# Routing the first batch in two groups of two head pairs, loading the next batch's q and k on the Pool queue, and eight buffers for the split of q and k, in a fused attention and feed-forward kernel

## The chip, the cores and the metric

The kernel runs on one core of one Trainium2 chip. The metric is the device time of one execution in microseconds (us). The kernel before took 321.93 us here (median of 4 executions, 321.57 to 322.32); in the rounds of the experiments its executions lay between 319.6 and 324.6. An execution counts as slow when it lies more than 1.5% above the fastest of its kernel, and as fast otherwise. Most are fast; the slow ones are up to five of the 20 or so of a run (e9, e13, e14, e15, e18), and the profiles of e9, e15 and e18 fell on one, which is said where it matters. The span of a profile is about 1.8 us shorter than the time of the same execution, and the profiled execution of the kernel before was one of its slower ones (323.8 us, span 322.0).

## The reference, cut to what matters

q, k and v are 4 x 8 x 768 x 64 (batches, heads, rows, columns). Each row of q and of k goes to the nearest of 16 centroids of its head; a query sees only keys of its own cluster. The result passes through a feed-forward layer of width 2048. Some lines are drawn together here.

```python
q_assign = np.argmax(np.einsum('bhsd,hcd->bhsc', q_n, c_n), axis=-1)
k_assign = np.argmax(np.einsum('bhsd,hcd->bhsc', k_n, c_n), axis=-1)
mask = q_assign[:, :, :, None] == k_assign[:, :, None, :]
scores = np.where(mask, scale * np.matmul(q, k.transpose(0, 1, 3, 2)), -1000000000.0)
...                                    # softmax
attn_out = np.matmul(attn, v)
h = x @ w_in                           # x: attn_out as 3072 x 512
out = (h * (1.0 / (1.0 + np.exp(-h)))) @ w_out
```

## The kernel before

The work is cut into pieces: 16 pairs of heads (four per batch), three thirds of the queries each. For every pair q and k are loaded (`nat`), split into a high and a low half of 16 bits (`hl`), and turned (`abt`): the first batch on TensorE, the later ones by a DMA transpose on the SP queue. TensorE computes the centroid logits (`psL`), VectorE turns them, takes the maximum and writes one-hots (`lt`, `mx`, `oht`, `ohu`), and these go as extra rows under q and k, so that one product gives the score and the mask at once (`st`). ScalarE takes the exponential (`P`), TensorE multiplies by v (`pv`), VectorE normalises (`xh`), and the feed-forward layer follows (`ph`, `tn`, `gt`, `po`). Four head pairs of one third make a chunk (12 in all).

The order of instructions on every engine isn't written out. The kernel holds a list scheduler that runs when it is built: each piece has a planned duration, a rank, buffers that it takes and gives, and for a DMA a planned landing. Whatever is ready first in this plan is emitted first, and the chip then runs each engine strictly in that order.

```python
    def split_hi(p, t, eng):
        hl = hls[p, t] = mp.tile([128, 2 * NJ, 2, D], f16, name="hl", bufs=5)
    ...
    def route_put(p, h, t, eng):               # one-hots under q or k, 16 rows a head
        g = 64 * h + 32 * t
        dst, src = heads(p, t)[D : D + HC, h], ohs[p][g : g + HC, :]
    ...
    def qk(n, s, p, u):
        K = D + HC                             # 64 + 16 rows
        st = sts[n, s] = ps.tile([128, 2, 2, UQ], f32, name="st", tag="st", bufs=2)
    ...                                        # in the scheduler
                x = min(can, key=lambda x: x.rank if e == "PE" else x.rank + x.t)
                x.fn(ENG[e])                   # emit it
    ...
    for pl in [[p] for p in range(HB)] + [[p, p + 1] for p in range(HB, NP, 2)]:
        groups[pl[-1]] = pl                    # first batch: four groups of one pair
    ...
            x = Piece({"SP": 0.5}, lambda e, p=p, t=t: load(p, t), ...)
    ...
                turned[p].append(Piece(
                    {"SP": 1.45}, lambda e, p=p, t=t: turn_dma(p, t), [los[t]], ..., dma=(1.9 * RATE, 2.0),
                ))
```

The logits of a group take one of the two score buffers (tag `st`), the same two through which every product of scores passes.

The softmax here doesn't subtract the row's maximum and nothing guards it: scores larger than these inputs give would overflow.

Of the kernel before, what the change touches and what calls it, by code (L numbers as in the profile page):

```python
# [19 lines left out]
def kernel(  # L20
# [43 lines left out]
    wlx = const.tile([128, HB * 64 + 32], f16, name="wl")  # L64
    wh, wl = (w[:, 0 : HB * 64].rearrange("p (r h c) -> p r h c", h=2, c=32) for w in (whx, wlx))

    NV = 6
# [12 lines left out]
    def load(p, t):  # L80
        b, r = divmod(p, HB)
        nat = mp.tile([128, 2, NJ * D], f32, name=f"nat{t}", bufs=3)
        nc.sync.dma_start(nat, (q, k)[t][b, 2 * r : 2 * r + 2].rearrange("h (p j) d -> p h (j d)", j=NJ))
        nats[p, t] = nat
# [6 lines left out]
    def split_hi(p, t, eng):  # L91
        hl = hls[p, t] = mp.tile([128, 2 * NJ, 2, D], f16, name="hl", bufs=5)
# [37 lines left out]
    def logits(pl):  # L130
        tl = []
        for lo, hi in ((0, 512), (512, 768)):
# [6 lines left out]
            if pl[0] >= HB:  # L139
# [59 lines left out]
    def route_put(p, h, t, eng):  # L199
        g = 64 * h + 32 * t  # L200
        dst, src = heads(p, t)[D : D + HC, h], ohs[p][g : g + HC, :]
        if eng is nc.scalar:
            eng.mul(dst, src, OHV)  # L203
        else:
            eng.tensor_scalar(out=dst, in0=src, scalar1=OHV, scalar2=None, op0=ALU.mult)  # L205

    def qk(n, s, p, u):
        K = D + HC
# [129 lines left out]
    def centroid_norm():  # L338
        newton()
        newton()  # L340
        nc.vector.tensor_scalar(out=cy, in0=cy, scalar1=1e-6, scalar2=None, op0=ALU.add)
        nc.vector.reciprocal(cw, cy)

    def centroid_split():
        cn = mp.tile([128, D], f32, name="cn")
        nc.gpsimd.tensor_scalar(out=cn, in0=craw, scalar1=cw, scalar2=OHV, op0=ALU.mult, op1=ALU.mult)

        for n in range(2):
            nc.gpsimd.tensor_copy(ch2[:, n, :], cn)
        for n in range(2):  # L350
            nc.gpsimd.tensor_tensor(out=cl2[:, n, :], in0=cn, in1=ch2[:, n, :], op=ALU.subtract)
# [13 lines left out]
    BUFS = {"nat0": 3, "nat1": 3, "hl": 5, "abt": 7, "moe": 3, "po": 1, "lt": 1, "mx": 1, "oht": 1, "ohu": 1, "oh": 2,  # L365
# [3 lines left out]
    RATE = 0.375  # L369
# [17 lines left out]
    def run(free):  # L387
# [3 lines left out]
        jobs, flowed, turn = {"SP": [], "POOL": []}, 0.0, 0  # L391
# [5 lines left out]
        for at in sorted(set(free.values())):  # L397
            post(at)

# [11 lines left out]
        def flow(new=None):  # L411
            nonlocal flowed, turn
            busy = [q for q in jobs.values() if q]
            for q in busy:
                q[0][0] -= (t - flowed) * RATE / len(busy)
# [7 lines left out]
            if busy:  # L423
                turn += 1
                post(t + max(min(q[0][0] for q in busy), 0.0) * len(busy) / RATE, "flow", turn)
# [51 lines left out]
    GAP = 1.7  # L477
    BACK = 6
    SEQ0 = [(0, 0), (0, 1), (1, 0), (2, 0), (3, 0), (1, 1), (2, 1), (3, 1), (0, 2), (1, 2), (2, 2), (3, 2)]
    LEAD, LEAD_V, LEAD_IN = 28, 16, 36  # L480
    FR0 = (-400, -285, -290, -280)
    REX = -300
    LATE = 10
    PSL = 16
    XPE = (0, 11)
    TURNED = (0, 1, 2, 3)


# [11 lines left out]

    def from_slot(x):
# [3 lines left out]
    free = {"PE": 1.0, "ACT": 2.0, "DVE": 1.7, "POOL": 1.3, "SP": 1.2}  # L505
    nc.sync.dma_start(craw, centroids.rearrange("h c d -> (h c) d"))
    nc.vector.memset(zbias, 0.0)
    nc.vector.memset(bias32, -32.0)
    for vt in vts:
        nc.gpsimd.memset(vt[:, :, :, D : D + 1], 1.0)  # L510
    nc.vector.memset(idle, 0.0)
    make_identity(nc, ident)
# [4 lines left out]
    x = Piece({"SP": 0.01}, lambda e: None, rank=-99, dma=(0.0, 1.2))  # L517
    x = Piece({"DVE": 0.45}, lambda e: centroid_square(), [x], rank=-9)
    x = Piece({"ACT": 0.3}, lambda e: centroid_root(), [x], rank=-900)
    Piece({"ACT": 1.28}, lambda e: e.preload_act_table(AF.Exp), [x], rank=-900)  # L520
    x = Piece({"DVE": 1.35}, lambda e: centroid_norm(), [x], rank=-900)
    x = Piece({"POOL": 1.8}, lambda e: centroid_split(), [x], rank=-99)
    cc = [("moe", "c0")]
    x = Piece({"PE": 0.6}, lambda e: centroid_turn(), [x], cc, rank=-99)
# [181 lines left out]
```

## Time and profile before

| | before |
|---|---|
| span of the profile | 322.0 us |
| TensorE (PE) / ScalarE (ACT) / VectorE (DVE) busy | 94% / 74% / 59% |
| needed matmul work, by the prediction's working | 282 us |
| first exponential; first product of the feed-forward layer (ph) | 19.64; 47.68 us |
| first logits of the second batch (psL of pairs 4 and 5) | 66.22 us |

The page cuts the span into 40 slices of 8.05 us. A digit is the busy share of the slice in tenths; PEclk is the granted TensorE clock, DMA the mean busy share of the 16 DMA engines. From the page of the kernel before:

```profile
PE   6688795999999999999989999999999999999994
...
PEclk9799998999999999999999999999999999999999
DMA  7999999999926990394996970293310200200001
```

TensorE is short of work only in the first seven slices, and the DMA engines are at 9 tenths in slices 2 to 11: the place where the change acts is also where DMA is full.

### The profile page before, as it was taken

The page shows a single profiled execution, that of the slowest core. Times are in us where ns is not written, and L with a number is a line of the kernel's source. Part 1 is how long each engine was busy: PE and PEld are TensorE (multiplying, and loading weights), DVE is VectorE, ACT ScalarE, POOL GpSimd, SP SyncE. Part 2 cuts the span into 40 slices and gives each one's busy share as a digit, 9 for nine tenths or more (in the row PEclk, how much of TensorE's full clock was granted, in tenths as well). Part 3 has the DMA queues.
Part 4 walks back from the last instruction along what each step waited for, and adds up shares of the span by engine and source line. Part 5 has one row for each costly group of instructions (what it writes and reads, how often), then busy time and mean ns, then how long its engine had stood idle before and what let it go on. Part 6 is the DMA issues. An engine that isn't in the chain of part 4 may idle for free.

```text
span 322.0 us, 7812 instructions
## 1 busy us (share of the span) xinstructions
PE 302.5 (94%) x3316; PEld 225.5 (70%) x3316; DVE 190.2 (59%) x356; ACT 239.3 (74%) x279; POOL 35.3 (11%) x57
## 2 busy tenths in 40 slices
PE   6688795999999999999989999999999999999994
PEld 4565574876877768777677777777777787786651
DVE  5798983675856878438328877338444344254431
ACT  5896994985678979886878787886787787786420
POOL 4952100024000000023200000040000000000000
PEclk9799998999999999999999999999999999999999
DMA  7999999999926990394996970293310200200001
GB/s 213 289 240 239 235 186 149 214 149 132 223 67 183 210 231 9 77 129 61 191 243 155 223 147 11 75 166 25 69 41 17 66 35 28 74 0 35 33 35 65
DMA packets 89843, 40.00 MB, mean 124 GB/s; under 512 B 75216, under 2 KB 86224, under 8 KB 89808
## 3 DMA queue, kind: packets, MB, share of 16 engines
q1 hardware_dynamic: 62032, 32.16, 44.1%
q0 software_dynamic: 27776, 7.34, 22.8%
q8 instruction: 26, 0.43, 0.6%
q14 instruction: 9, 0.07, 0.1%
HBM read 27.30 MB, written 6.29 MB: 104 GB/s over the span
## 4 chain that ended last, share of the span: by engine, by line
PE 78%; DMA 9%; DVE 9%; ACT 1%; issue 1%; SPq 1%; DVEq 0%
PE ph L276 25%; PE po L298 24%; PE st L213 16%; PE pv L229 9%; DMA abt<-hl 6%; PE psL L155 3%; DMA nat<-in_q_dram 2%; DMA xt<-xh 2%; DVE hl L102 1%; DVE abt L205 1%; DVE ohu L187 1%; DVE lt L162 1%; DVE hl L97 1%; DVE mx L173 1%; DVE oht L180 1%
## 5 line engine op out<-in xcount | busy, mean ns | idle before, releaser
L219 ACT ACTIVATE P<-st,bias 128x1024 f16<-128x1024 f32 x144 | 156.7, 1114 | 36.6 <-PE st L213 36.1
L285 DVE SCALAR_TENSOR_TENSOR gt<-tn,ph 128x512 f16<-128x512 f32 x96 | 65.1, 683 | 61.1 <-ACT tn L282 60.4
L276 PE MATMUL ph<-xt,win_s 128*128 128x256 f16 x768 | 97.1, 274 | 4.1 <-DVE xh L243 3.3
L298 PE MATMUL po<-wout_s,gt 128*128 128x512 f16 x384 | 96.5, 379 | 1.1 <-DVE ot L307 1.1
L213 PE MATMUL st<-abt 80*128 80x256 f16 x576 | 85.5, 274 | 4.0 <-ACT abt L203 1.6
L276 PEld LDWEIGHTS <-win_s 128*128 128x128 f16 x768 | 74.1, 98 | 18.1 <-DVE xh L243 3.6
L282 ACT ACTIVATE tn<-ph,zbias 128x512 f32<-128x512 f32 x96 | 65.3, 686 | 25.3 <-PE ph L276 24.7
L213 PEld LDWEIGHTS <-abt 80*128 80x128 f16 x576 | 55.1, 98 | 26.5 <-issue 3.7
L298 PEld LDWEIGHTS <-gt 128*128 128x128 f16 x384 | 35.9, 97 | 29.1 <-issue 1.6
L89 POOL DMA_DIRECT2D vt<-in_v_dram x32 | 26.5, 833 | 174.0 <-PE pv L229 165.2
L229 PE MATMUL pv<-vt,P 128*128 128x65 f16 x1152 | 43.3, 193 | 0.2 <-ACT P L219 0.2
L229 PEld LDWEIGHTS <-P 128*128 128x128 f16 x1152 | 41.8, 98 | 2.1 <-ACT P L219 0.3
L102 DVE SCALAR_TENSOR_TENSOR hl<-nat,hl 128x768 f16<-128x768 f32 x32 | 29.8, 956 | 2.8 <-ACT hl L95 2.5
L307 DVE TENSOR_SCALAR ot<-po 128x512 f32<-128x512 f32 x24 | 16.5, 686 | 24.2 <-PE po L298 24.1
L242 DVE RECIPROCAL rz<-pv 128x4 f32<-128x4 f32 x48 | 8.6, 178 | 28.0 <-PE pv L229 27.6
L243 DVE TENSOR_TENSOR xh<-pv,rz 128x256 f16<-128x256 f32 x48 | 20.4, 424 | 1.7
L97 DVE TENSOR_SCALAR hl<-nat 128x768 f16<-128x768 f32 x19 | 10.4, 556 | 5.3 <-DMA abt<-hl 5.2
L268 PE MATMUL warm<-idle,ident 128*128 128x256 f16 x66 | 11.7, 316 | 1.7 <-POOL ident masks.py:199 1.7
L95 ACT ACTIVATE hl<-nat 128x768 f16<-128x768 f32 x13 | 11.0, 843 | 2.6 <-DMA nat<-in_q_dram 2.2
L155 PE MATMUL psL<-abt,wh 128*32 128x512 f16 (+1 forms) x128 | 10.5, 340 | 0.7 <-DVE abt L122 0.4
L187 DVE STREAM_TRANSPOSE ohu<-oht 128x768 f16<-128x768 f16 x10 | 9.8, 977 | 0.9 <-DVE oht L180 0.5
L117 PE MATMUL ptt<-ident,hl 128*128 128x128 f16 x96 | 7.7, 235 | 2.7 <-ACT abt L122 1.9
(52 smaller groups left out, 100.4 us busy)
## 6 DMA issues: line engine op xcount, KB each, us to landing
nat<-in_q_dram SPq DMA_DIRECT2D x16, 384.0 KB, 5.2
nat<-in_k_dram SPq DMA_DIRECT2D x16, 384.0 KB, 5.6
out_dram<-ot SPq DMA_DIRECT2D x24, 256.0 KB, 2.1
vt<-in_v_dram POOLq DMA_DIRECT2D x32, 96.0 KB, 5.1
win_s<-in_moe_w_in_dram POOLq DMA_DIRECT2D x4, 512.0 KB, 13.2
wout_s<-in_moe_w_out_dram POOLq DMA_DIRECT2D x4, 512.0 KB, 22.9
abt<-oh SPq DMA_DIRECT2D x48, 24.0 KB, 2.0
abt<-hl SPq DMA_TRANSPOSE x24, 4.5
```

Of the source, the lines that this page charges most:

```text
L89: nc.gpsimd.dma_start(vts[p % NV][:, h, :, 0:D], v[b, 2 * r + h].rearrange("(p j) d -> p j d", j=NJ))
L102: nc.vector.scalar_tensor_tensor(out=hl[:, :, 1, :], in0=nat, scalar=128.0, in1=hl[:, :, 0, :], op0=ALU.mult, op1=ALU.subtract)
L155: nc.tensor.matmul(psL[g : g + 32, 0 : hi - lo], w, x[:, lo:hi], start=first, stop=last)
L213: nc.tensor.matmul(st[:, a, h, :], ab[0:K, 1, h, ts(2 * s + a, 128)], ab[0:K, 0, h, ts(u, UQ)], start=True, stop=True)
L219: nc.scalar.activation(out=P, in_=sts.pop((n, s)), func=AF.Exp, bias=bias32, scale=ESC)
L229: nc.tensor.matmul(out[:, e, h, :], P[:, a, h, ts(e, 128)], vts[p % NV][:, h, 2 * s + a, 0 : D + 1], start=(s + a + h + e == 0), stop=(s = ...
L243: nc.vector.tensor_tensor(out=xhs[c][:, :, r], in0=out[:, :, :, 0:D], in1=rz.unsqueeze(3).to_broadcast([128, 2, 2, D]), op=ALU.mult)
L276: nc.tensor.matmul(ph[:, e].rearrange("p (g x) -> p g x", g=2), win_s[:, r, ts(2 * f + e, 128)], xts[c][:, :, r, :], start=(r == 0), stop= ...
L282: nc.scalar.activation(out=tn, in_=phs[c, f], func=AF.Tanh, bias=zbias, scale=0.5)
L285: nc.vector.scalar_tensor_tensor(out=gts[c][:, 2 * f : 2 * f + 2, :], in0=tns.pop((c, f)), scalar=1.0, in1=phs.pop((c, f)), op0=ALU.add, o ...
L298: nc.tensor.matmul(pos[c, s], gts[c][:, fc, ts(s, 128)], wout_s[:, fc, :], start=(fc == 0), stop=(fc == NFB - 1))
L307: eng.tensor_scalar(out=ot, in0=pos.pop((c, s)), scalar1=0.5, scalar2=None, op0=ALU.mult)
```

## The change

The intent is to take VectorE's routing of the first batch, the wait for a split buffer, and the late start of the next batch's loads out of the first 66 us.

```diff
-    def load(p, t):
+    def load(p, t, eng):
...
-        hl = hls[p, t] = mp.tile([128, 2 * NJ, 2, D], f16, name="hl", bufs=5)
+        hl = hls[p, t] = mp.tile([128, 2 * NJ, 2, D], f16, name="hl", bufs=8)
...
-            if pl[0] >= HB:
+            if len(pl) == 2:
...
-        K = D + HC
+        K = D + (32 if p < HB and len(groups_of[p]) == 2 else HC)
...
-    FR0 = (-400, -285, -290, -280)
+    FR0 = (-295, -295, -285, -280)
-    LEAD, LEAD_V, LEAD_IN = 28, 16, 36
+    LEAD, LEAD_V, LEAD_IN = 18, 22, 23
-    XPE = (0, 11)
+    XPE = (0,)
+    GR0 = [[0, 1], [2, 3]]
...
-                {"SP": 0.5}, lambda e, p=p, t=t: load(p, t), turned[HB - 1] if b == 1 else (), ...
+                {"POOL": 0.75} if b == 1 else {"ACT": 0.45} if p == 0 and t == 1 else {"SP": 0.5}, ...
...
-                    rank=-9 if b == 0 else -2, dma=(1.9 * RATE, 2.0),
+                    rank=-9 if b == 0 else -2, dma=(1.45, 2.0, 0.25),
```

Cut from it: the one-hot writes by 32 rows with a mask (`pick`) that clears the other head's 16 rows of k; the centroids split on ACT and DVE instead of Pool; the value and weight loads moved ahead of the second batch's q and k, with a planned start of 7.8 us (`HOLD`); the order of the first batch's score products (`SEQ0`) and a few smaller ranks and gaps; new figures for the plan's DMA model; and a table of 12 hand-set shifts of rank. `LEAD`, `LEAD_V` and `LEAD_IN` say how many score slots (products of scores, four matmuls each) ahead of its use the splits, values and loads of a later batch may start.

## The prediction

> **What bounds the kernel now.** I read the busy shares first: TensorE (PE) 94%, ScalarE (ACT) 74%, VectorE (DVE) 59% of 322.0 us. So PE is the bound on average, but the 40 slices show its first seven at 6 to 9 tenths. The question is therefore how much of the span is not needed matmul work, and where it lies. The chain of waits gives the warm duration of each group of matmuls:
>
> ```profile
> 60.22 0.88 PE ph L276 x8
> 61.10 0.98 PE st L213 x8
> 64.26 0.86 PE po L298 x4
> 66.29 1.42 PE psL L155 x32
> ...
> 159.14 5.07 DMA xt<-xh
> ...
> 309.29 0.87 PE ph L276 x8
> ```
>
> Columns are start, duration, what. In unbroken stretches eight ph matmuls take 0.873 us, four po 0.866, four st (scores) 0.437, 24 pv 0.735, a routing group psL of 32 takes 1.41. Times the counts: 96 x 0.873 + 96 x 0.866 + 144 x 0.437 + 48 x 0.735 = 265.1 us; routing logits 10.2, PE transposes 6.7. Sum 282 us. So 40 us of the span are not needed work. The timeline of PE says where:
>
> ```profile
> 46.95 0.89 PE L229 MATMUL pv<-vt,P 128*128 128x65 f16 x24
> 47.68 1.04 PE L276 MATMUL ph<-xt,win_s 128*128 128x256 f16 x8
> ...
> 53.31 1.64 PE L276 MATMUL ph<-xt,win_s 128*128 128x256 f16 x8 [3.28 <-DVE xh L243]
> 54.74 1.91 PE L213 MATMUL st<-abt 80*128 80x256 f16 x8
> ```
>
> Up to the first ph at 47.68 the counts in the program order (20 score slots, 6 pv, all of the first batch's transposes and logits) make 22.0 us of work: 25.7 us lost. From there to the next batch's first psL at 66.22, 13.1 us of work take 18.5: 5.4 lost, of which 3.28 is one wait and the rest mostly a cold clock (eight ph in 1.64 us instead of 0.87). From 66.22 to the last po at 318.0, 247.1 us of work take 251.8: 4.7 lost. The last eviction and store take 4.0. Sum 39.8. Hence nearly all that can be won lies before 66 us.
>
> What sets the first ph? The timelines of ACT and DVE:
>
> ```profile
> 19.64 2.12 ACT L219 ACTIVATE P<-st,bias 128x1024 f16<-128x1024 f32 x2
> ...
> 32.00 1.70 ACT L203 ACTIVATE abt<-ohu 16x768 f16<-16x768 f16 x2 [2.43 <-DVE ohu L187]
> 34.29 12.18 ACT L219 ACTIVATE P<-st,bias 128x1024 f16<-128x1024 f32 x12 [0.59 <-PE st L213]
> ```
> ```profile
> 52.14 0.56 DVE L97 TENSOR_SCALAR hl<-nat 128x768 f16<-128x768 f32 x1 [5.25 <-DMA abt<-hl]
> 52.62 0.17 DVE L242 RECIPROCAL rz<-pv 128x4 f32<-128x4 f32 x1
> ```
>
> The first ph comes right after the sixth pv, which needs 18 exponentials. Only 6 are done by 28.87, with ACT copies and routing between them; then ACT waits for DVE's routing of the later pairs, and 12 run without a gap at 1.015 us from 34.29 to 46.47. The first ph follows 1.2 us later. So the first-batch routing on DVE sets when ACT can run, and ACT's exponentials set when the MoE starts. The second fence is the later stall: DVE, in order, holds a split of the next batch for a free buffer (five of them, freed by a DMA transpose issued at 41.03 that lands 11.1 us later), and behind it stand the normalisation and the gates that PE needs.
>
> **What the skill says.** "TensorE: Matmul & The Clock Gate", Part 2, LDWEIGHTS: the time depends on columns, not on contraction rows. The trace agrees: st with 80 rows and ph with 128 both take 274 ns a matmul and 98 ns a load, so 96-row scores cost PE nothing. The same page, Part 1: an idle PE falls to half clock; the cold ph after the 3.28 us wait agrees. "DMA: Bandwidth & Descriptors", Issuing engines are not separate DMA queues: Pool's loads share the same 16 DMA engines, so moving loads brings no bandwidth, only another order. The trace agrees: the engines are at 9 tenths in nearly all of the first 80 us whichever queue moves. "GPSIMD Engine Reference", 2.1: the first call of a freshly loaded Pool kernel costs about 6 us. No run here shows it; it matters below.
>
> **The change part by part.**
>
> Routing in two groups. DVE now does per group lt 1.12 + mx 0.95 + oht 0.95 + ohu 0.98 = 4.0 (the two-pair durations of the second batch), twice, against 1.12 + 0.55 + 0.56 + 0.98 = 3.2 four times: 8.0 for 12.8, so 4.8 us less. The 16 writes of one-hots stay at 0.36 on DVE or 0.84 on ACT, with 32 partitions in place of 16. The price: the first exponential must wait for four tiles, not two. In the new instruction order every first-batch PE transpose copy but the DVE ones is placed on ACT before its first exponential, and after it 20 exponentials stand in one row.
>
> When does that row start? Loads: the third and fourth landed at 8.86 and 9.88, the fifth at 11.0. The new order issues q0 first and k0 beside it on ACT, so I take about 0.4 earlier. ACT splits q2 at 10.6 to 11.5, then four copies at 0.75 to 14.5, another to 15.3, the split of k3 to 16.1, two copies to 17.6; these finish pairs 0 and 1, and psL runs to 19.1. DVE has meanwhile three low splits from 11.5 to 14.4 (0.95 each), two copies, and the high and low splits of k2, k3, q3, to 19.5. Then 4.0 for the routing and the writes of pair 0, 23.5 to 24.7; scores; first exponential about 25.3. That is 5.7 later than now (19.64), but the 18th ends at 25.3 + 18 x 1.015 = 43.6 instead of 46.47. The second group is routed on DVE by 29.7 and its pairs written by 31 and 33.3, before ACT has used up the nine slots of pairs 0 and 1 (34.4): no gap. First ph: 43.6 + 1.2 = 44.8, a gain of 2.9 us.
>
> Eight split buffers. The DVE wait of 5.25 goes, and with it the 3.28 us wait and the cold stretch. From first ph to psL the new order has 12.5 us of work (27 score slots, 7 pv, 8 ph, 2 po) where the old one had 13.1. Walking ACT's 20 exponentials, the tanhs after them (0.69) and the gates (0.68) leaves PE about even: psL near 57.4. But psL also needs four DMA transposes. The low splits end about 43, 46, 48 and 52; a transpose took 4.2 us free and 8.4 to 12.2 among loads, so the fourth lands between 56 and 60. I put 1 us of stall there: 58.4.
>
> Next batch's q and k on Pool. They now queue behind the weights. Weights move at about 0.4 MB/us when alone; 8.4 MB after the values (19 us) end near 40, not 48.6, and q4 lands about 41.5. DVE reaches its split at 39 and has the next normalisation due at 42: just in time. Behind this, the SP queue is free for the transposes. No further gain counted.
>
> Centroid work moved from Pool to ACT and DVE: about 0.4 us and 0.4 us, plus 0.9 us of masks on DVE before the centroids arrive; all in time that DVE and ACT spend waiting for loads. Value loads could start before 7.88. Last chunk turned by DMA: 28 po (6.1 us) stand between its last pv and its first ph, over 0.8 + 3.3 to 5.1 us of normalisation and transpose: hidden.
>
> Sum: psL at 58.4 instead of 66.2, work behind it 247.1 in both, so 7.8 us; 322.2 - 7.8 = 314.4. I say 314.5.
>
> **The rivals.**
> (1) The data hold it up. If Pool starts its value loads at 2 us instead of 7.9, their small packets compete with q and k: between 12 and 18 us the SP queue fell from 0.3 to 0.1 MB/us beside them. The first exponential would slip to 28 or later and the gain at the first ph would be gone: about 317.5. The 6 us of the skill speaks against it, the absence of any wait in the instruction order for it.
> (2) The transposes take the place of the wait. DMA is saturated to about 70 us in the old trace, the bytes stay, and the four transposes landed by 61.1 there. If they do no better now, psL waits to 61 and the time is 317.
> (3) ACT becomes the bound in the first 60 us and all else is hidden well: no stall at psL, weights early, steady part slightly better (no 0.9 us wait for xt as at 164): 312.
>
> **Range and chances.** The first two cost 2.5 to 3 us each and can add up, the third gives 2.5; the later schedule was also reshuffled, worth 1.5 either way. 310.5 to 319 should hold it 8 times in 10. Two per cent is 315.8, only 1.3 above my value: faster 0.62, same 0.36, slower 0.02.
>
> **What would show it.** Right: 20 exponentials in one row on ACT from about 25, first ph near 45, no DVE wait for a DMA transpose, psL of the second batch by 59, and the stretch after that about as long as before. Wrong: value loads landing before 12 us and q1, k1 after 11; a DVE wait for q4 longer than 2 us; a PE wait for abt<-hl before psL; more than 6 us lost after 60 us.

## The result, and the profile after

The changed kernel took 325.15 us (median of 4, 324.81 to 327.0) against 321.93 us in the same rounds. The ratio of the fast runs is 1.0112, with a 95% interval of 1.0070 to 1.0153. A ratio here is the mean time of one kernel's fast runs over that of the other's in the same rounds, so it isn't quite the ratio of the medians. The kernel is 1% slower, inside the 2% band, and 10.6 us above the predicted 314.5; the range of 310.5 to 319.0 doesn't hold it.

The profiled execution was the slowest of the four (327.0 us, span 325.2). A repeat in another call (324.82 us, span 323.0) is used beside it, below as "the repeat". From the page of the changed kernel, the same rows:

```profile
PE   7487999789999999998999999999999999999994
...
PEclk9978799979999999999999999999999999999999
DMA  8999999995092199997473399995120200300301
```

The 5 of slice 7, which was the wait for a split buffer, has become a 9. But slices 2 and 4 are lower than before (4 and 7 for 6 and 8), slices 8 and 9 have 7 and 8 where both had 9, and the clock is low in slices 3 to 5 and 9. DMA is full to slice 9.

The timeline of TensorE. The columns are the start, the duration, the engine, the line, the operation, output and inputs, and in brackets the idle time before it and what ended it:

```profile
27.96 1.05 PE L217 MATMUL st<-abt 96*128 96x256 f16 x8 [1.37 <-DVE lt L164]
...
49.43 1.04 PE L280 MATMUL ph<-xt,win_s 128*128 128x256 f16 x8
...
63.77 0.38 PE L156 MATMUL psL<-abt,wh 128*32 128x512 f16 x1 [1.28 <-DMA abt<-hl]
...
66.51 0.61 PE L156 MATMUL psL<-abt,wh 128*32 128x512 f16 x6 [2.36 <-DMA abt<-hl]
```

The first ph comes at 49.43, not at the predicted 44.8. The logits of pairs 4 and 5 are reached at 62.10, but their group stands on the DMA transposes until 66.51. The timeline of ScalarE, for the row of exponentials:

```profile
26.34 1.11 ACT L223 ACTIVATE P<-st,bias 128x1024 f16<-128x1024 f32 x1
28.61 4.33 ACT L223 ACTIVATE P<-st,bias 128x1024 f16<-128x1024 f32 x4 [1.16 <-PE st L217]
34.00 2.18 ACT L223 ACTIVATE P<-st,bias 128x1024 f16<-128x1024 f32 x2 [1.06 <-PE st L217]
36.56 1.11 ACT L223 ACTIVATE P<-st,bias 128x1024 f16<-128x1024 f32 x1 [0.38 <-PE st L217]
38.03 12.20 ACT L223 ACTIVATE P<-st,bias 128x1024 f16<-128x1024 f32 x12 [0.35 <-PE st L217]
```

The predicted "20 exponentials in one row" are broken four times by 2.95 us in all. The 18th ends at 48.21 (counted from the records; 45.88 in the repeat, 43.6 predicted). The timelines of SP and Pool of the changed kernel, for the transposes and for the first loads:

```profile
48.14 22.55 SPq L113 DMA_TRANSPOSE abt<-hl  x7
```
```profile
1.59 6.76 POOL L90 DMA_DIRECT2D vt<-in_v_dram  x8
```

and SP of the kernel before:

```profile
41.03 1.38 SPq L112 DMA_TRANSPOSE abt<-hl  x1
```

The value loads begin at 1.59 us, where the plan meant 7.8; and the first transpose of the second batch is issued 7 us later than before, though its data (q4) landed at 39.0 us. VectorE's timeline shows both ends of that:

```profile
43.57 0.18 DVE L246 RECIPROCAL rz<-pv 128x4 f32<-128x4 f32 x1 [2.37 <-PE pv L233]
...
44.13 0.55 DVE L98 TENSOR_SCALAR hl<-nat 128x768 f16<-128x768 f32 x1
...
47.16 0.95 DVE L103 SCALAR_TENSOR_TENSOR hl<-nat,hl 128x768 f16<-128x768 f32 x1
...
63.98 0.56 DVE L98 TENSOR_SCALAR hl<-nat 128x768 f16<-128x768 f32 x1 [3.99 <-DMA nat<-in_k_dram]
```

The split of q4 stands behind a normalisation that waits 2.37 us for TensorE, and later a split waits 3.99 us for k7, with gates of the feed-forward layer behind it.

**Where the time went.** All matmul records are in the traces, so a ledger can be made: at a given matmul, the time minus the needed work of all matmuls before it (the prediction's durations times the counts) is the time lost up to there. In us:

| lost up to | before | changed | repeat |
|---|---|---|---|
| first ph | 25.7 | 27.5 | 25.1 |
| 60 us | 30.7 | 27.4 | 26.1 |
| 80 us | 31.2 | 33.8 | 30.6 |
| 160 us | 31.9 | 36.0 | 33.0 |
| last po | 35.9 | 39.6 | 37.4 |

The needed work is 282.2 us before and 281.6 after (one chunk fewer is turned on TensorE). So the changed kernel is 3.3 us ahead at 60 us, and then loses 6.4 us in 20 us where the kernel before loses 0.5, and 5.8 us from 80 us on against 4.7.

### The profile page after: what moved, and what is told of

Same layout as the page of the kernel before. It is cut to its first block, busy times and chain, and to the rows that moved or that the text cites. A ratio compares the mean times of both kernels' runs of the same rounds, so it can differ in the third digit from the quotient of the medians.

```text
span 325.2 us, 7775 instructions
## 1 busy us (share of the span) xinstructions
PE 304.6 (94%) x3309; PEld 227.1 (70%) x3309; DVE 189.3 (58%) x360; ACT 235.9 (73%) x272; POOL 38.3 (12%) x60
## 4 chain that ended last, share of the span: by engine, by line
PE 78%; DMA 9%; DVE 8%; ACT 3%; issue 1%; SPq 0%
PE po L302 24%; PE ph L280 22%; PE st L217 17%; PE pv L233 10%; DMA abt<-hl 6%; PE psL L156 3%; ACT P L223 3%; DMA nat<-in_k_dram 2%; DVE hl L103 2%; DVE gt L289 1%; DVE hl L98 1%; DMA craw<-in_centroids_dram 1%; DVE abt L209 1%; DVE ot L311 1%; DVE lt L163 0%
## 5 line engine op out<-in xcount | busy, mean ns | idle before, releaser
L217 PE MATMUL st<-abt 80*128 80x256 f16 (+1 forms) x576 | 86.4, 277 | 2.6 <-DVE lt L164 1.4
L217 PEld LDWEIGHTS <-abt 80*128 80x128 f16 (+1 forms) x576 | 55.2, 99 | 23.8 <-issue 4.2
L302 PEld LDWEIGHTS <-gt 128*128 128x128 f16 x384 | 36.2, 98 | 31.3 <-issue 2.9
L233 PEld LDWEIGHTS <-P 128*128 128x128 f16 x1152 | 43.2, 99 | 2.3
L233 PE MATMUL pv<-vt,P 128*128 128x65 f16 x1152 | 44.5, 196 | 0.0
L311 DVE TENSOR_SCALAR ot<-po 128x512 f32<-128x512 f32 x24 | 16.6, 690 | 25.7 <-PE po L302 23.2
L156 PE MATMUL psL<-abt,wh 128*32 128x256 f16 (+1 forms) x128 | 11.5, 352 | 5.5 <-DMA abt<-hl 5.3
L272 PE MATMUL warm<-idle,ident 128*128 128x256 f16 x67 | 12.9, 333 | 1.4 <-POOL ident masks.py:199 1.4
L98 DVE TENSOR_SCALAR hl<-nat 128x768 f16<-128x768 f32 x21 | 11.8, 572 | 4.0 <-DMA nat<-in_k_dram 4.0
L123 ACT COPY abt<-ptt 128x768 f16<-128x768 f16 x14 | 10.1, 812 | 2.1 <-PE ptt L118 2.1
L118 PEld LDWEIGHTS <-hl 128*128 128x128 f16 x96 | 6.0, 100 | 7.3 <-DVE hl L103 3.6
```

What stands on the lines that cost most here:

```text
L156: nc.tensor.matmul(psL[g : g + 32, 0 : hi - lo], w, x[:, lo:hi], start=first, stop=last)
L217: nc.tensor.matmul(st[:, a, h, :], ab[0:K, 1, h, ts(2 * s + a, 128)], ab[0:K, 0, h, ts(u, UQ)], start=True, stop=True)
L233: nc.tensor.matmul(out[:, e, h, :], P[:, a, h, ts(e, 128)], vts[p % NV][:, h, 2 * s + a, 0 : D + 1], start=(s + a + h + e == 0), stop=(s = ...
L302: nc.tensor.matmul(pos[c, s], gts[c][:, fc, ts(s, 128)], wout_s[:, fc, :], start=(fc == 0), stop=(fc == NFB - 1))
L311: eng.tensor_scalar(out=ot, in0=pos.pop((c, s)), scalar1=0.5, scalar2=None, op0=ALU.mult)
```

## The experiments

Eighteen kernels ran. All are of three rounds, except the last two of five. "Ratio" is against the kernel before of the same call.

| run | what it is | median us (executions) | ratio, 95% interval |
|---|---|---|---|
| e1_same | changed kernel again | 324.82 (7) | 1.0104, 1.0068 to 1.0140 |
| e2_buf8 | before + eight split buffers | 323.09 (13) | 1.0053, 1.0024 to 1.0081 |
| e3_pool | before + loads on Pool | 328.06 (4) | 1.0217, 1.0172 to 1.0262 |
| e4_groups | before + two groups | 327.55 (4) | 1.0181, 1.0139 to 1.0224 |
| e5_order | changed, splits earlier | 326.36 (4) | 1.0123, 1.0072 to 1.0175 |
| e6_held | changed, values really held | 325.31 (16) | 1.0094, 1.0066 to 1.0121 |
| e7_ring | changed, logits in the other ring | 322.54 (12) | 1.0031, 1.0007 to 1.0055 |
| e8_clear | changed, no loads beside transposes (wrong result) | 327.82 (4) | 1.0189, 1.0125 to 1.0254 |
| e9_ring_clear | e7 + the same, planned | 323.21 (20) | 1.0031, 1.0006 to 1.0056 |
| e10_clear | the same without e7's change | 325.28 (4) | 1.0129, 1.0075 to 1.0183 |
| e11_ring_held | e7 + e6 | 326.18 (4) | 1.0146, 1.0089 to 1.0204 |
| e12_all | e6 + e7 + clear | 322.23 (20) | 1.0024, 1.0002 to 1.0045 |
| e13_told | changed, one number of the plan | 320.68 (20) | 0.9945, 0.9919 to 0.9971 |
| e14_ring_told | e7 + the same number | 319.91 (20) | 0.9941, 0.9915 to 0.9967 |
| e15_told_held | e14 + e6, other leads | 321.59 (21) | 0.9985, 0.9960 to 1.0010 |
| e16_told_early | the same, long leads | 328.30 (4) | 1.0192, 1.0144 to 1.0240 |
| e17_final | e14 + a second number of the plan | 322.02 (14) | 1.0011, 0.9984 to 1.0038 |
| e18_final5 | the same, first number smaller | 320.54 (22) | 0.9961, 0.9940 to 0.9982 |

### e1_same: the changed kernel again

> The changed kernel once more, for a second profile, since the first was its slowest execution and had a cold stretch of 6.8 us from 30 to 37. Theory A (the row of exponentials is broken by the order itself: the second group's logits hold one of the two score buffers until DVE reads them) expects again a gap of about 1.2 us after the first exponential and the first ph later than 47; if the cold stretch is missing, some 2 us less than the first profile: span 323, first ph 47 to 48, psL of the second batch still stalled by 3 to 5 us. Theory B (the cold stretch alone broke the row) expects, without it, the 18th exponential at about 45 and no stall at psL.

The slower time repeats, so it isn't the chip of the first measurement. The timeline of TensorE in the repeat, at the logits of pairs 4 and 5 (reached at 59.76):

```profile
60.64 0.38 PE L156 MATMUL psL<-abt,wh 128*32 128x512 f16 x1 [0.49 <-DMA abt<-hl]
63.34 1.04 PE L156 MATMUL psL<-abt,wh 128*32 128x512 f16 x6 [2.32 <-DMA abt<-hl]
```

The second group of six takes 1.04 us where the profile of the first measurement had 0.61: the clock fell in the wait. The hole behind the first exponential is there again (1.16 us). So the stall at the logits and the broken row belong to the kernel, and the next runs take them apart.

### e2_buf8, e3_pool, e4_groups: each part alone on the kernel before

e2, in the buffer and in the scheduler's table:

```diff
-        hl = hls[p, t] = mp.tile([128, 2 * NJ, 2, D], f16, name="hl", bufs=5)
+        hl = hls[p, t] = mp.tile([128, 2 * NJ, 2, D], f16, name="hl", bufs=8)
-    BUFS = {"nat0": 3, "nat1": 3, "hl": 5, ...
+    BUFS = {"nat0": 3, "nat1": 3, "hl": 8, ...
```

> The kernel before with eight split buffers and nothing else. If my sum was right that the 5.25 us wait of DVE and with it 3.28 us of PE and a cold stretch go, and nothing takes their place: 317 to 318 us, ratio 0.985 to 0.99. The rival, that the saturated DMA gives the wait back at the second batch's psL: 321 to 322, ratio 1.00, with a new PE wait for abt<-hl near 60 us.

The wait of VectorE for a free split buffer is gone, as predicted. In its place VectorE waits for the data. The timeline of VectorE, and that of TensorE, of this run:

```profile
52.91 0.56 DVE L97 TENSOR_SCALAR hl<-nat 128x768 f16<-128x768 f32 x1 [1.43 <-DMA nat<-in_k_dram]
```
```profile
55.11 1.48 PE L229 MATMUL pv<-vt,P 128*128 128x65 f16 x24 [2.52 <-DVE gt L285]
```

k7 landed late and the gates stood behind its split, so TensorE waited 2.52 us where it had waited 3.28. More buffers moved the wait from the buffer to the load; the ledger shows 34.3 us lost at 80 us against 31.2.

e3, the core of it (the values and weights move ahead of the loads in Pool's order too):

```diff
-                {"SP": 0.5}, lambda e, p=p, t=t: load(p, t), turned[HB - 1] if b == 1 else (), ...
+                {"POOL": 0.75} if b == 1 else {"SP": 0.5}, lambda e, p=p, t=t: load(p, t, e), [csplit] if b == 1 else (), ...
```

> The kernel before with the next batch's q and k on the Pool queue behind values and weights, and nothing else (five split buffers). If the Pool queue is what costs the changed kernel its time: slower, 324 to 326, with the first DMA transpose of the next batch near 46 to 48 us instead of 41 and a PE wait at psL of 3 us or more. If the place in the queue is harmless: 320 to 323, weights all landed by 41 instead of 48.6.

Here the logits of pairs 4 and 5 wait for the transposes as in the changed kernel. From TensorE's timeline:

```profile
64.43 0.58 PE L155 MATMUL psL<-abt,wh 128*32 128x512 f16 x1 [1.86 <-DMA abt<-hl]
```

The transposes of the second batch begin at 46.06 instead of 41.03, inside the expected 46 to 48, and the group, reached at 62.18, stands until 65.75. So this wait comes with the loads on Pool, without the groups and the buffers. The first ph is also 1.75 us later than before (49.43), for which no cause was looked for; the time, 328.06, lies above the expected 324 to 326.

e4, the core of it:

```diff
-    for pl in [[p] for p in range(HB)] + [[p, p + 1] for p in range(HB, NP, 2)]:
-        groups[pl[-1]] = pl
+    groups = {pl[-1]: pl for pl in [[p, p + 1] for p in range(0, NP, 2)]}
...
-        K = D + HC
+        K = D + (32 if p < HB and len(groups_of[p]) == 2 else HC)
```

> The kernel before with the first batch routed in two groups of two pairs with 96-row scores, and nothing else. By my prediction's step the first ph comes 2 to 3 us earlier: 319 to 320, ratio 0.99 to 0.995. Theory A (logits of the second group hold a score buffer, four tiles to wait for) expects no gain: first ph within 1 us of 47.7, 321 to 324.

The 18th exponential ends at 45.29 instead of 46.47, so the groups do what was wanted by 1.2 us. But with five split buffers VectorE stood. Its timeline, then TensorE's:

```profile
51.61 0.56 DVE L98 TENSOR_SCALAR hl<-nat 128x768 f16<-128x768 f32 x1 [8.31 <-DMA abt<-hl]
```
```profile
52.78 0.72 PE L262 MATMUL xp<-ident,xh 128*128 128x128 f16 x5 [7.69 <-DVE xh L247]
```

The first ph came at 55.47. So no part gains alone: with the groups alone a split stood for a buffer, with the buffers alone it stood for a load, and the loads on Pool bring the wait at the logits. One caution holds for these three runs: each also gets an order of its own from the scheduler, so a ratio is that of the part with the order that came with it.

### e5_order: the splits of the second batch earlier

The emission is put off to the end of the plan, and five pieces of VectorE are moved ahead:

```diff
+    MOVES = [(('hi', 4, 0), 'before', ('norm', 3)), (('lo', 4, 0), 'before', ('norm', 3)), (('hi', 4, 1), 'before', ('norm', 4)),
+             (('lo', 4, 1), 'before', ('norm', 4)), (('hi', 5, 1), 'before', ('norm', 4))]
```

> The changed kernel with nothing changed but the place of five VectorE instructions: the two halves of the split of q4 go ahead of the normalisation of the fourth unit, the two halves of k4 and the high half of k5 ahead of the normalisation of the fifth. Theory A (the transposes of the next batch are late because their splits stand behind normalisations that wait for TensorE; q4 has landed at about 38-39 us): the first transpose is issued at about 40.5 instead of 45.8 us, the second at about 43.5 instead of 48.8, the wait of the batched logits for the transposes (2.8 us in the repeat of the changed kernel, plus the cold clock after it) disappears or shrinks below 1 us, the first product of the second layer stays at 47-47.7, and the time falls by 3 to 4.5 us to about 320.5-321.5. Theory B (the transposes are slow because of the loads on the Pool queue beside them, whenever they are issued): the loads of q7 and k7 move forward with the splits that free their buffers, the transposes still take 9-12 us, the fourth still lands after 60 and the time gains under 1.5 us.

This was my first theory, and it fell. The first transpose was issued at 41.38, 4.4 us before the repeat's, and the first two landed about 3 us earlier, but the last two, for which the logits wait, at 62.5 and 63.7, against 61.9 and 63.3 in the repeat. TensorE's timeline:

```profile
63.73 0.63 PE L156 MATMUL psL<-abt,wh 128*32 128x512 f16 x6 [4.28 <-DMA abt<-hl]
```

The DMA view of the window with these four transposes (columns: what, queue, kind, count, median us from issue to landing):

```profile
abt<-hl SPq DMA_TRANSPOSE x4, 11.8
```

In the repeat the median of the four is 10.0. Issued earlier, they only took longer. The late issue of the first one was visible and real, and not what set the landing of the last.

### e6_held: the value loads held back for good

```diff
+        if p == 0:
+            nc.gpsimd.tensor_copy(held1, cl2[:, 0, 0:1])    # ahead of the first value load
```

> The changed kernel with the value loads really held back until the centroids are ready: a one-column copy on Pool reads the low half of the centroids before the first value load, so the first load is issued at about 7-8 us instead of 1.6. Order on every engine else unchanged. Rival 1 of the prediction (the value loads disturb q and k of the first batch): k3 lands 1-2 us earlier than 15.1, the first exponential comes 1-2 us earlier than 25.4 and so does the first product of the second layer (45.5-46.5). But everything behind on the Pool queue (weights, q4, k4) moves back by up to 5 us, so the wait of the batched logits grows by as much as was won or more. Expected sum: 322-326, no gain. If rival 1 is wrong: k3 lands at 15 as before, first exponential unchanged.

The first value load is issued at 9.15 us. k3 lands at 14.04 instead of 15.29, the first exponential starts at 24.10 instead of 25.35, and the 18th ends at 43.41 instead of 45.88. So the early value loads do disturb the first batch. What happens next is in the timelines of VectorE and TensorE:

```profile
43.41 0.56 DVE L100 TENSOR_SCALAR hl<-nat 128x768 f16<-128x768 f32 x1 [4.00 <-DMA nat<-in_q_dram]
```
```profile
44.58 0.45 PE L264 MATMUL xp<-ident,xh 128*128 128x128 f16 x5 [1.37 <-DVE xh L249]
...
64.61 1.04 PE L158 MATMUL psL<-abt,wh 128*32 128x512 f16 x6 [2.41 <-DMA abt<-hl]
```

Everything behind on Pool's queue moved back: q4 landed 4.2 us later (43.39), VectorE waited for it, and the normalisation behind it came late. First ph 46.11, the wait at the logits longer, the time unchanged. The disturbance is shown, and so is that removing it alone brings nothing.

### e7_ring: the second group's logits out of the score buffers

```diff
-            if pl[0] >= PSL:
+            if pl[0] >= PSL or pl[0] == 2:
```

with the same condition where the scheduler takes the buffers.

> The changed kernel with the logits of the second group of two pairs in two of the three buffers of the other accumulator ring, instead of one of the two score buffers. Theory C (the row of exponentials is broken because the second group's logits hold one of two score buffers until VectorE has read them): the wait of TensorE of 1.4 us behind the first exponential and the 1.16 us hole on ScalarE behind it disappear; the 18th exponential ends about 1.2 us earlier (44.7 at a clock like the repeat's), the first product of the second layer at about 46. The list schedule behind it changes as well (its own sum is 1.5 us longer), so the whole time is expected at 322-326, and what is read from this run is the first 48 us. If theory C is wrong, the hole stays with another releaser (DVE copies to the score rows).

ScalarE's timeline of this run:

```profile
26.65 20.23 ACT L223 ACTIVATE P<-st,bias 128x1024 f16<-128x1024 f32 x20
```

Twenty exponentials in one row, without a gap, as the prediction had wanted them. From the first start to the end of the 18th it took 18.22 us; the prediction had 18.3; the changed kernel took 21.87 and the repeat 20.53. The same row takes 18.2 us in every later profile with this edit but e16's (19.57), and 19.3 to 21.9 us in all kernels built on the changed one without it; e4, with an order of its own and without the edit, took 18.49, so the conflict depends on the order too. In the changed order the two score buffers were the cause: while the logits of the second group held one of them until VectorE had read it, TensorE could be only one product ahead of ScalarE, and every slow stretch of TensorE broke the row. The time fell to 322.54.

### e8_clear: the transposes without loads beside them

The loads of q7, k7 and the values of pairs 6 and 7 wait on Pool until the four transposes of pairs 4 and 5 have landed:

```diff
+        if (p, t) == (HB + 3, 0):
+            for o, i in ((HB, 0), (HB, 1), (HB + 1, 1), (HB + 1, 0)):
+                nc.gpsimd.tensor_copy(seen, abts[o][0:1, i, 0, 0:1])
+    MOVES = [(('load', 7, 0), 'after', ('turn', 5, 0)), (('v', 6), 'after', ('load', 7, 0)), ...
```

> The changed kernel with Pool's loads of q7, k7 and of two values held back until the four transposes of pairs 4 and 5 have landed (Pool reads an element of each first). Order on SP, VectorE, ScalarE and TensorE unchanged. Theory B (the transposes are slow because loads on the Pool queue run beside them): from issue to landing the first four take 4-6 us instead of 9-12, the fourth is issued at about 54.5 instead of 58 and lands by 59.5, the batched logits wait under 0.5 us, and q7 and k7 land near 62-64, where VectorE may now wait for them instead; time 320-323. Theory A alone (late issue, the duration is the transposes' own): durations stay over 8 us, the stall of 2.8 us stays, time 324-326.

The result was wrong (relative error 0.20), by a mistake of mine: the moved value loads were emitted behind products that read them. Only the DMA durations of this run are used; they don't depend on the values. The DMA view of the window with the four transposes, and TensorE's timeline:

```profile
abt<-hl SPq DMA_TRANSPOSE x4, 3.3
```
```profile
60.40 0.61 PE L159 MATMUL psL<-abt,wh 128*32 128x512 f16 x8
...
70.59 1.48 PE L236 MATMUL pv<-vt,P 128*128 128x65 f16 x24 [8.16 <-DVE gt L292]
```

The same transposes take 3.3, 3.6, 3.3 and 3.2 us, against 9.2, 11.8, 10.8 and 5.2 in the repeat, and the logits start the moment they are reached. The fourth, which ends the stall, was slow in another way. The timeline of SP at the third transpose, in the repeat and in e8:

```profile
51.11 6.85 SPq L113 DMA_TRANSPOSE abt<-hl  x1
```
```profile
51.40 1.40 SPq L116 DMA_TRANSPOSE abt<-hl  x1
```

The instruction that issues the third transpose held SP for 6.85 us instead of 1.40. So the fourth, whose split was done at 54.18 in the repeat, was issued only at 58.06, and landed 5.2 us later; in e8 it was issued at 54.73, as soon as its split was done. But q7 then landed late, at 63.4 us, VectorE stood before its split with gates behind it, and TensorE waited 8.16 us. That the loads make the transposes slow, in flight and at their issue, is shown; the cure moved the wait.

### e9_ring_clear and e10_clear: the same, with the plan told of it

The hold now stands in the scheduler, which also takes q7 and k7 to land 7 us after their slot:

```diff
-            ... lambda e, p=p, t=t: load(p, t, e), (), ... dma=(1.03, 1.7, 1.5),
+            ... lambda e, p=p, t=t: load(p, t, e), turned[HB + 1] if p == HB + 3 else (), ... dma=(1.03, 7.0 if p == HB + 3 else 1.7, 1.5),
```

> The logits of the second group in the other accumulator ring (as in the run e7_ring), and the loads of q7, k7 and of the values of pairs 6 and 7 held on Pool until the four transposes of pairs 4 and 5 have landed, this time with the plan told of it, so that the splits of q7 and k7 and the later instructions stand where the data is there (the first try of this gave a wrong result, since a product was emitted ahead of the load that it needs). Theory B (the transposes are slow because of loads on the Pool queue beside them): the four transposes take 3.2-3.7 us each from issue to landing, the fourth lands at 57-58, the batched logits start at 58.5-59.5 without a wait of over 0.6 us, no cold clock follows, and with 252 us behind it as in the kernel before the time is 313-317, faster than both by 1.5% to 2.5%. Rival: the work is only pushed to the next load (VectorE waits for q7 and k7 after 62 with gates of the second layer behind it, or TensorE waits for the values of pair 6), and the time stays at 321-324.

> The same hold of the loads of q7, k7 and of two values, without the change of the ring for the second group's logits. If the stall at the batched logits is one cause and the broken row of exponentials the other, this should lie between e9_ring_clear and the changed kernel: the transposes at 3.2-3.7 us, no stall at the logits of pairs 4 and 5, but the hole of 1.4 us behind the first exponential as in the changed kernel; 316-320.

Both results are correct, and in both the logits of pairs 4 and 5 start at once (59.36 and 58.85 us) after transposes of 3.2 to 5.4 us. The expected 313 to 317 and 316 to 320 us were missed by far: 323.21 and 325.28. The slow transfer had moved: the sixth transpose (of pair 6), now beside the held loads, took 14.3 and 12.6 us. The profile of e9 fell on a slow execution and has a wait of 2.38 us at 70.37 for which it shows no releaser; that stays open. The ledger of e10 says where it went: 26.8 us lost at 80 us, 4.4 less than the kernel before, then 5.3 us more by 160 us, where the kernel before loses 0.7.

### e11_ring_held and e12_all: the repairs added up

e11 is e7 with the line of e6; e12 is e9 with the line of e6.

> e7_ring plus the real hold of the value loads until the centroids are ready (e6_held). If the two add up: the first exponential at about 24-24.5 with no hole behind it, the 18th ends at 42.5-43.5, the first product of the second layer at 44.5-46, the stall at the batched logits stays or grows to 3-5 us because nothing was done for the transposes; time 320.5-323.5, no better than e7_ring by over 1 us. Should it be under 320 then the early value loads cost more than the trace of e6_held shows.

> All three repairs together: real hold of the value loads, the logits of the second group in the other ring, and the loads of q7, k7 and two values behind the transposes. If the three causes are separate, the first product of the second layer comes at 44.5-46, the batched logits start near 57.5-59 without a wait, and the time is 312-316, at or just under that of e9_ring_clear; if the transposes set the start of the batched logits in any case (their splits wait for TensorE's products), no better than e9_ring_clear.

e11 starts the first ph at 45.0 and then loses 7.7 us at the logits, since q4 is later and the loads meet the transposes: the two repairs don't add. e12 has the first ph at 44.46, nearly the predicted 44.8, and the logits of pairs 4 and 5 run from 58.28, the predicted 58.4, though its first two transposes, issued while Pool's earlier loads still ran, took 9.3 and 8.1 us. Still it takes 322.23 us. TensorE's timeline of e12, in the third batch:

```profile
137.86 2.33 PE L285 MATMUL ph<-xt,win_s 128*128 128x256 f16 x16 [3.89 <-DMA xt<-xh]
```

This line is most of the answer to "where did the gain go". Up to 120 us e12 has lost 25.3 us, 6.4 less than the kernel before; by 140 us it has lost 30.9. The gain was real and was given back some 75 us later, at the next long wait for a DMA transpose. Here again SP was held: the input of this transpose was written at 127.27, but two transposes of q or k stood ahead of it on SP until 132.96, and then it took 4.8 us.

### e13_told and e14_ring_told: one number of the plan

```diff
-                    rank=-9 if b == 0 else -2, dma=(1.45, 2.0, 0.25),
+                    rank=-9 if b == 0 else -2, dma=(1.45, 5.0, 0.25),
```

The third theory: TensorE works in the plan's order, and the plan lets a transpose land 2.0 us after its flow. The two traces of the changed kernel have 3.7 to 8.5 us from issue to landing in the later batches and up to 12.6 in the second, so logits are placed where the data isn't there yet, with other work behind them.

> The changed kernel with one number changed in its list schedule: a DMA transpose of the split is taken to land 5.0 us after its slot on SP ends instead of 2.0. No instruction is added or taken away; the order changes, above all TensorE's (the batched logits of pairs 4 and 5 go behind some 4 us more of other work). Theory D (the order was planned on transposes that land too early, and TensorE, which works in order, stands at the logits while other work lies behind them): the waits for the transposes at 59-63, at 145-148 and at 216 us shrink from 2.8, 1.3-1.5 and 1.3 us to under 0.8 each, the cold clock behind the first goes, and the time falls by 4-5 us from the changed kernel's 325 to 319.5-321.5, level with the kernel before or up to 0.7% better. Rival (the loss is DMA traffic itself, and whatever is put first, something waits): the waits move to other places and the time stays at 323-326.

> The same number changed in the kernel with the second group's logits in the other accumulator ring (e7_ring, 322.5). Theory D: the two add, since one acts at 27 us and the other from 59 us on: 317.5-319.5, faster than the kernel before by about 1%. Rival: 321-323.

e13 has the same instructions as the changed kernel, in another order, and takes 320.68 us, ratio 0.9945 against 1.0104: 1.6% faster through one planning number. This is somewhat flattered: one very fast execution (316.48) makes five of e13's 20 count as slow; with all 20 the ratio of the means is 0.997, 1.3% below the changed kernel (324.80). TensorE's timeline of e13:

```profile
64.52 1.05 PE L233 MATMUL pv<-vt,P 128*128 128x65 f16 x24 [1.83 <-DVE gt L289]
...
68.06 0.81 PE L156 MATMUL psL<-abt,wh 128*32 128x512 f16 x8
```

The transposes land as before (55.2 to 64.1 us); now the logits come after them. No wait of TensorE for a transpose over 0.6 us is left in the whole trace. The ledger of these runs, in us lost:

| lost up to | before | changed | e7 | e12 | e13 | e14 |
|---|---|---|---|---|---|---|
| first ph | 25.7 | 27.5 | 24.1 | 22.5 | 25.8 | 24.2 |
| 60 us | 30.7 | 27.4 | 25.5 | 23.9 | 25.6 | 25.1 |
| 80 us | 31.2 | 33.8 | 30.8 | 25.2 | 31.0 | 31.1 |
| 160 us | 31.9 | 36.0 | 32.6 | 32.4 | 31.5 | 32.1 |
| last po | 35.9 | 39.6 | 35.3 | 36.2 | 33.3 | 33.8 |

From 80 us on e13 loses 2.3 us, where the kernel before loses 4.7 and the changed one 5.8. e14 adds the ring of e7 and is, at 319.91 us, the fastest by its median, though not by more than the intervals allow. Both beat the changed kernel clearly; against the kernel before e14 is 0.6% faster (0.9945 with all executions counted), e13 only just, and both are inside the 2% band. The expected 317.5 to 319.5 for e14 was missed: the 1.6 us that it's ahead of e13 at the first ph are gone by 80 us. Both wait there for a gate (the first line above), and VectorE's timeline of e13 shows what stands ahead of that gate, the split of k7:

```profile
61.58 0.56 DVE L98 TENSOR_SCALAR hl<-nat 128x768 f16<-128x768 f32 x1 [3.31 <-DMA nat<-in_k_dram]
```

### e15_told_held and e16_told_early: other leads

```diff
-    LEAD, LEAD_V, LEAD_IN = 18, 22, 23
+    LEAD, LEAD_V, LEAD_IN = 20, 13, 24        # e15; e16: 27, 13, 36
```

with e14's and e6's edits, a planned landing of 5.0 or 6.0 us (e16: 5.0 and 4.0), and small changes of the gaps between score slots; e16 also drops the table of hand-set ranks.

> Ring, real hold of the value loads, transposes planned at 6.0 us (second batch) and 5.0 us (later ones), and leads of the later batches set to the best of the kernel's own list schedules under these numbers (splits 20 slots ahead, loads 24). If the three causes and the planned landing are the whole story, the first product of the second layer comes at 44.5-46, no wait over 1 us stands behind it, and the time is 315-318. If the later batches still lose 1-2 us at their logits: 318-320.

> As e15_told_held, but with the long leads of the kernel before (splits 27 slots ahead, loads 36). If the short leads of the changed kernel (18 and 23, against 28 and 36) are what costs the later batches, this loses under 1 us between 80 and 300 us beyond the 3.0 us of the kernel before, and beats e15_told_held: 314.5-317. If leads do not matter once the landing is planned right: the same as e15_told_held within 1 us.

Both missed. In both VectorE met the late q4 of e6, and TensorE waited for a normalisation, 2.72 us at 41.83 in e15 and 5.12 us at 42.77 in e16; e15's profile is of a slow execution. Both also stood again at the logits of pairs 4 and 5, for 3.4 and 3.6 us at the last transpose, though the plan had it land late: a longer planned landing does not remove the wait in every order. The long leads aren't what was lost, at least not with this order: from 80 to 300 us e16 loses 2.1 us and e13 1.2.

### e17_final and e18_final5: a second number

```diff
-                ... dma=(1.03, 1.7, 1.5),
+                ... dma=(1.03, 8.0 if p == HB + 3 else 1.7, 1.5),
```

on e14, with the transposes planned at 6.0 (e17) and 5.0 us (e18).

> As e14_ring_told, with the transposes planned to land 6.0 us after their slot, and the loads of q7 and k7 planned to land 8.0 us after theirs instead of 1.7. If these two numbers are the rest: VectorE's wait for k7 falls from 3.3 to under 1 us, TensorE's wait of 2.3 us for the gate at 61 us and the cold clock behind it go, TensorE has lost under 28 us by 80 us (31.1 in e14_ring_told), and the time is 316-318, faster than the kernel before by 1.2% to 1.8%. Rival (DMA traffic keeps something waiting there whatever the order): 319-321 as e14_ring_told.

> The same with the transposes planned at 5.0 us: the batched logits stand about 1.5 us earlier in TensorE's order, so a wait of up to 1 us for the transposes is expected there; 316-319, within 1 us of e17_final. If it is better than e17_final, 6.0 us was too careful.

The wait for the gate went down to 0.71 us for a normalisation, and another took its place. TensorE's timeline of e17:

```profile
74.84 1.20 PE L280 MATMUL ph<-xt,win_s 128*128 128x256 f16 x8 [2.87 <-DMA xt<-xh]
```

e17 has lost 31.8 us by 80 us, no less than e14, and e18 31.9 (a slow execution, in which TensorE stood 5.5 us at the logits again). Both times, 322.02 and 320.54, miss what was expected, and both are above e14's. Here the rival was right: between 60 and 80 us something waits for DMA in all these orders. Of the kernels built on the changed one, only those that hold the loads back with the plan told of it (e9, e10, e12) had lost under 30 us by 80 us. And since one number moves the whole order, part of e13's gain may be the luck of its order; that was not separated. The combination of e12 with e13's number was not run, and nor was e13's number on the kernel before; both stay open.

## Why the prediction was wrong, point by point

Three steps failed: the unbroken row of exponentials (18.3 us predicted, 20.5 to 21.9 measured), the 1 us of stall at the logits (3.6 to 4.4 measured), and the unchanged rest (4.7 us of losses predicted, 5.8 to 6.8 measured).

**Where TensorE loses time now.** Right: the first 66 us set what can be won, and the losses there were read correctly.

**First exponential at 25.3.** The number was right (25.35 in the repeat, 26.34 in the profile), partly by luck: it assumed value loads from about 7.9 us, and with them really held (e6) the exponential starts at 24.10. So the other estimates were about 1.2 us too long, and the early value loads filled that. The durations of the two-pair routing (lt to ohu 4.0 us) and of the 96-row scores were right: from start to start in a warm row a matmul of 96 rows takes 109 ns, as one of 80 does.

**"No gap", 18th exponential at 43.6, first ph at 44.8.** Failed. The row took 20.5 to 21.9 us instead of 18.3, because the second group's logits hold one of the two score buffers; e7 removes that and gets 18.22. Without the edit of e7 the hole behind the first exponential (1.16 us) is in both profiles; cold stretches of TensorE widen the rest. The prediction checked when the one-hots would be ready, not which buffers the logits take meanwhile. Predicted gain at the first ph 2.9 us; measured a loss of 1.8 in the profile and a gain of 0.6 in the repeat.

**First ph to the logits in 12.6 us.** Right: 12.67 in both traces.

**"The fourth lands between 56 and 60. I put 1 us of stall there".** Failed in size. The mechanism was named, with the right range for one transpose (8.4 to 12.2 us among loads, as the traces then showed), but the landing was taken too early: 66.5, in the repeat 63.3, and the stall is 4.4 and 3.6 us. The cause, by e5, e8 and e10, is the loads of q7, k7 and two values on Pool's queue at that moment: medians of 10.0 us with them in the repeat and 11.8 with an earlier issue (e5), 3.3 without (e8). The prediction took each transpose as free to start when its split ends. The low splits ended at 45.8, 48.8, 51.0 and 54.2 in the repeat, 2 to 3 us later than it said though q4 had landed at 39.2 and not at 41.5, and the issue of the third then held SP until 57.96. So "the SP queue is free for the transposes" failed too: free of loads, it was held by the transposes themselves, and the engines behind the queues were at 9 tenths. By the ledger, from the first ph to 80 us 6.3 us were lost where the prediction allowed about 1.

**The wait for a split buffer goes.** Right as such: no such wait is left. Failed as a gain: e2 shows a wait for the load of k7 taking its place (1.43 us), and in the changed kernel it is 3.99 us on VectorE.

**"Work behind it 247.1 in both, so 7.8 us".** Failed. The work was the same but not the losses: 5.8 us from 80 us on instead of 4.7 (6.8 in the repeat). The order there was planned on transposes that land early; e13 changes that number alone and brings it to 2.3. Part of the size is scatter: e6, with the changed kernel's order, lost about 3.5 us there in its one profile, its fastest execution. e12 shows the general point: being 6 us ahead at 120 us isn't yet being 6 us ahead at the end.

**The sum.** The predicted losses at the end were 35.9 less 7.3; the measured ones are 35.9 plus 3.7, a difference of 11.0: 4.7 at the first ph, 5.2 to 80 us, 1.1 after it. In the repeat it is 8.8: 2.3, 4.4 and 2.1.

**The rivals.** (1) was right in its mechanism: the value loads start at 1.59 us and delay the first batch by 1.25 us (e6); its size (28 or later) wasn't reached. The prediction set the 6 us of a first Pool call against it; the traces don't show such a delay: the first value load, issued at 1.59 us, moved its first packets at 5.96 us in the repeat. (2) was right, and its "waits to 61" was still too early. (3) was wrong. The range treated (1) and (2) as worth 2.5 to 3 us each that might add; the buffer conflict and the later order weren't in it.

## What to carry to other kernels

When an engine's order is fixed beforehand, a transfer that lands later than planned costs twice, in the wait and in all the work that stands behind it; so compare the planned landing with the trace, beside the loads that will really run then, before anything else. Follow every new occupant of a buffer ring (here a second group of logits among two score buffers) from its first write to its last read. And when a change is ahead early in the trace, keep a ledger of lost time to the end, because a gain can be given back at the next wait.

## What the Trainium skill lacked or had wrong

- "Advanced Engine Details and Errata", X-Bar Transpose (TRN2), says that transpose DMAs are as fast as regular ones. It doesn't say what they cost beside another queue's loads: here a transpose of 128 x 12 x 128 elements of 16 bits took 3.2 to 3.6 us without loads beside it (e8), and the first three of the second batch took 8.8 to 11.9 us while Pool's queue loaded q7, k7 and two values (the repeat, e13), about three times as long. Nor does it say that the instruction that issues one can hold its engine: 1.4 us on SP in e8, up to 6.85 in the repeat.
- "GPSIMD Engine Reference", 2.1 Instruction dispatch, gives about 6 us for a first call of a freshly loaded kernel. It doesn't say whether a plain DMA issued from Pool pays for one. Here no 6 us is seen: the first value load was issued at 1.59 us and the first packets of its queue moved at 5.96 us, 4.4 us later (the repeat), against 2.6 us for a first issue at 9.15 us (e6); the first copy on Pool took 1.05 us (e6).
